# Sinkhorn-sorted block attention and a two-layer dense block: loading one batch at a time, and placing attention inside the second dense layer

## The chip, the cores and the metric

The kernel runs on one core of a Trainium2 chip. The time is what the device needs for one execution, in microseconds (us); three runs gave 297.11, 297.15 and 297.39. Beside these stands one profiled execution, whose trace gives every instruction's start and length. Five engines work side by side: TensorE (PE; matmuls and transposes, with the loading of their weights shown apart as PEld), VectorE (DVE), ScalarE (ACT), GpSimd (POOL) and SyncE (SP). Each has its own queue and waits on the others through semaphores.

## The reference

There are 4 batches of 8 heads with 768 tokens of 64 numbers. A head's tokens form 8 blocks of 96. A small 8x8 matrix per head is exponentiated and normalized along rows and columns, five times (Sinkhorn); it mixes the blocks of k and of v; then each block of queries attends to its mixed block alone. The heads side by side form a 3072 x 512 matrix x that goes through two dense layers.

```python
for _ in range(5):
    P = P - np.max(P, axis=-1, keepdims=True)
    P = np.exp(P)
    P = P / (np.sum(P, axis=-1, keepdims=True) + 1e-09)
    P = P / (np.sum(P, axis=-2, keepdims=True) + 1e-09)
k_sorted = np.einsum('bhij,bhjcd->bhicd', P, k_b)      # v likewise
scores = scale * np.matmul(q_b, k_sb.transpose(0, 1, 2, 4, 3))
attn = softmax(scores)                                  # rows, max taken off
x = (attn @ v_sb), heads side by side                   # 3072 x 512
h = x @ w_in                                            # 512 -> 2048
g = s * (np.maximum(h, 0.0) ** 2) + b
out = g @ w_out                                         # 2048 -> 512
```

## The kernel before

All matmuls take bf16; the loads issued by POOL narrow fp32 to bf16 on the way. The four batches are handled as two groups of two. `load_raw` (L74 on) brings a group's q, k and v in with one partition for each (batch, head, block): 128 partitions, a block's 96 x 64 numbers in each. After group 0 the whole of w_in (L94) and the whole of w_out (L96) are loaded, all on POOL's queue.

The Sinkhorn loop (L123 to L140) alternates between DVE and ACT. `build_pd` spreads the result into `pd`, a 128 x 128 block-diagonal mixing matrix. `transforms(g)` cuts the rest into pieces:

- `qk_piece` (L196): per token offset in a block one pair of matmuls, with the raw rows as weights, turns q (with the identity) and k (with `pd`) into "head dimension on partitions", 64 columns each; the PSUM result is copied to SBUF by `evac`, which alternates DVE (L171) and ACT (L173).
- `v_piece` (L206): per head-dimension index one matmul with 96 weight columns, taken with a stride of 64 elements, and 128 moving columns.

`attention` handles half a batch, 4 blocks of all 8 heads, which is one dense tile of 384 tokens: per pair of heads `s_piece` (scores, L229, exponential on ACT, L233) and `p_piece` (values with a column of ones for the row sum, L248; reciprocal and scaling on DVE, L253 and L254), and last `t_piece` (transposes of x, L265, and a copy to `xt`).

The dense layers: `ffn1(t)` computes 16 chunks of 128 hidden columns, two at a time (L290: 8 matmuls of 384 columns), then relu on ACT (L295) and the square on DVE (L296). `ffn2(t)` computes three blocks of 128 rows, each of 16 matmuls of 512 columns (L304), an output step on DVE (L307) that applies s and the bias, and a store by SP (L310). The bias row is b times the column sum of w_out: POOL adds the 16 slices (L326, L328), one matmul with ones spreads the sum (L330), DVE scales it (L332).

The order: group 0's transforms and its four halves of attention come first, then the bias, then `ffn1(0)`. After it `ffn1(t+1)` and `ffn2(t)` alternate, and a counter of slots (`slot`, one for each pair of chunks and each row block) runs group 1's pieces between them. The program's order is a priority; a scheduler at build time lays out each engine's queue, PE's too, from it. PSUM has two pools, `psa` (3 buffers of two banks) and `psb` (2 buffers of one bank).

Of the kernel before, what the change touches and what calls it, by code (L numbers as in the profile page):

```python
# [13 lines left out]
AX = mybir.AxisListType  # L14


@with_exitstack
def kernel(
# [12 lines left out]
    nc = tc.nc  # L31
# [5 lines left out]
    NG = 2  # L37
    GB = B // NG
# [7 lines left out]
    CH = BLK // 2  # L46
    VW = D + 2
    scale = float(D) ** -0.5

    raw = [t.rearrange("b h (j c) d -> (b h j) (c d)", j=NB) for t in (q, k, v)]  # L50
# [3 lines left out]
    wpool = ctx.enter_context(tc.tile_pool(name="wpool", bufs=1))  # L54
    rawp = ctx.enter_context(tc.tile_pool(name="rawp", bufs=1))
    trp = ctx.enter_context(tc.tile_pool(name="trp", bufs=1))
    atp = ctx.enter_context(tc.tile_pool(name="atp", bufs=4))
    xp = ctx.enter_context(tc.tile_pool(name="xp", bufs=2))
    xtp = ctx.enter_context(tc.tile_pool(name="xtp", bufs=5))
# [10 lines left out]
    nc.scalar.dma_start(out=s_bc, in_=moe_s.to_broadcast([128, 1]))  # L70
    b_bc = const.tile([128, 1], FP)
    nc.scalar.dma_start(out=b_bc, in_=moe_b.to_broadcast([128, 1]))

    def load_raw(g):  # L74
        rows = slice(g * 128, (g + 1) * 128)
        tiles = []
        for t, nm in enumerate("qk"):
            halves = []
            for hf in range(2):
                ti = rawp.tile([128, CH, D], BF, name=f"{nm}b{g}{hf}", tag=f"{nm}b{hf}")  # L80
                nc.gpsimd.dma_start(
                    out=ti.rearrange("p c d -> p (c d)"),
                    in_=raw[t][rows, hf * CH * D:(hf + 1) * CH * D])
                halves.append(ti)
            tiles.append(halves)
        vb = rawp.tile([128, BLK, D], BF, name=f"vb{g}", tag="vb")
        nc.gpsimd.dma_start(out=vb.rearrange("p c d -> p (c d)"), in_=raw[2][rows])
        tiles.append(vb)
        return tiles

    ident = const.tile([128, 128], BF)
    raws = [load_raw(0)]
    wi = wpool.tile([128, NHP, d_ff], BF)
    nc.gpsimd.dma_start(out=wi, in_=moe_w_in.rearrange("(hp p) f -> p hp f", p=128))  # L94
    wo = wpool.tile([128, NF, d_model], BF)
    nc.gpsimd.dma_start(out=wo, in_=moe_w_out.rearrange("(f p) n -> p f n", p=128))  # L96


    make_identity(nc, ident)
    identf = const.tile([128, 128], FP)  # L100
    nc.vector.tensor_copy(out=identf, in_=ident)
# [6 lines left out]
    emat = const.tile([BH, NG * 128], FP)  # L108
    nc.gpsimd.memset(emat, 1.0)
    nc.gpsimd.affine_select(out=emat, in_=emat, pattern=[[1, NG * 128]], base=0,  # L110
                            channel_multiplier=-NB, compare_op=ALU.is_ge, fill=0.0)
    nc.gpsimd.affine_select(out=emat, in_=emat, pattern=[[-1, NG * 128]], base=NB - 1,
                            channel_multiplier=NB, compare_op=ALU.is_ge, fill=0.0)
    onesf = const.tile([128, 128], FP)
    nc.gpsimd.memset(onesf, 1.0)
    jsel = const.tile([128, NB], FP)
    nc.vector.tensor_reduce(out=jsel, in_=identf.rearrange("p (m x) -> p x m", x=NB),
                            axis=AX.X, op=ALU.add)

# [3 lines left out]
    nc.vector.tensor_reduce(out=rstat, in_=sn, axis=AX.X, op=ALU.max)  # L123
    nc.vector.tensor_tensor(out=sn, in0=sn, in1=rstat.broadcast_to([BH, NB, NB]),
                            op=ALU.subtract)
    for it in range(5):
        nc.scalar.activation(out=sn, in_=sn, func=AF.Exp)
        nc.vector.tensor_reduce(out=rstat, in_=sn, axis=AX.X, op=ALU.add)
        nc.vector.reciprocal(out=rrec, in_=rstat)
        nc.vector.tensor_tensor(out=sn, in0=sn, in1=rrec.broadcast_to([BH, NB, NB]),  # L130
                                op=ALU.mult)
# [185 lines left out]
    for p in pieces:  # L317
        p()
# [82 lines left out]
```

## Time and profile before

| | us |
|---|---|
| median of three runs | 297.15 |
| the profiled execution, whole | 297.94 |
| its span, first to last instruction | 295.9 |
| PE busy | 245.7 |
| DVE busy | 117.1 |
| ACT busy | 104.1 |
| POOL busy | 27.9 |
| mean granted PE clock | 0.885 of full |

The page cuts the span into 40 slices of 7.4 us; a digit is the busy share in tenths. A row of a group gives line, engine, operation, output and inputs, shape and count, then busy time and mean length of one, then the idle time of the engine before it and what ended it. Matmuls overlap in the pipeline, so the mean length of one is longer than the distance between two; a distance is read from starts. A row of the timeline begins with the start and the length of a run of like instructions.

### The profile page before, as it was taken

The page shows a single profiled execution, that of the slowest core. Times are in us where ns is not written, and L with a number is a line of the kernel's source. Part 1 is how long each engine was busy: PE and PEld are TensorE (multiplying, and loading weights), DVE is VectorE, ACT ScalarE, POOL GpSimd, SP SyncE. Part 2 cuts the span into 40 slices and gives each one's busy share as a digit, 9 for nine tenths or more (in the row PEclk, how much of TensorE's full clock was granted, in tenths as well). Part 3 has the DMA queues.
Part 4 walks back from the last instruction along what each step waited for, and adds up shares of the span by engine and source line. Part 5 has one row for each costly group of instructions (what it writes and reads, how often), then busy time and mean ns, then how long its engine had stood idle before and what let it go on. Part 6 is the DMA issues. An engine that isn't in the chain of part 4 may idle for free.

```text
span 295.9 us, 5457 instructions
## 1 busy us (share of the span) xinstructions
PE 245.7 (83%) x2421; PEld 155.4 (53%) x2438; DVE 117.1 (40%) x220; ACT 104.1 (35%) x126; POOL 27.9 (9%) x42
## 2 busy tenths in 40 slices
PE   0474982005899999999999999999999999999994
PEld 0373972003675666558864565555465465455441
DVE  4763442003473455433533463434354255324221
ACT  2052261001654656305452364084054155046000
POOL 8100003993000000000000000000000000000000
PEclk9997555555555999999999999999999999999999
DMA  6999994299800000011001100100100110110111
GB/s 94 195 230 199 214 206 78 35 214 219 172 2 0 1 2 4 11 62 38 0 0 38 71 2 32 63 13 2 72 35 2 71 38 0 72 38 0 73 71 71
DMA packets 7847, 20.28 MB, mean 69 GB/s; under 512 B 912, under 2 KB 2960, under 8 KB 7568
## 3 DMA queue, kind: packets, MB, share of 16 engines
q0 software_dynamic: 4032, 13.63, 24.0%
q1 hardware_dynamic: 3504, 6.30, 5.7%
q8 instruction: 19, 0.31, 0.4%
q10 hardware_dynamic: 288, 0.00, 0.1%
q14 instruction: 4, 0.03, 0.0%
HBM read 27.27 MB, written 6.29 MB: 113 GB/s over the span
## 4 chain that ended last, share of the span: by engine, by line
PE 71%; ACT 3%; issue 2%; DVE 1%; ACTq 0%
PE hps L290 28%; PE ops L304 28%; PE tv L206 3%; PE pv L248 3%; PE sc L229 3%; PE tr L265 2%; PE tp L196 2%; ACT at L233 2%; ACT rt L295 1%; PE bps L330 1%; DVE ks L171 0%; DVE ot L307 0%; DVE gt L296 0%; ACT xt L173 0%; ACTq L233 0%
## 5 line engine op out<-in xcount | busy, mean ns | idle before, releaser
L290 PE MATMUL hps<-xt,wi 128*128 128x384 bf16 x512 | 91.5, 330 | 0.5 <-ACT rt L295 0.5
L304 PE MATMUL ops<-wo,gt 128*128 128x512 bf16 x367 | 83.7, 379 | 1.1 <-issue 0.5
L295 ACT ACTIVATE rt<-hps 128x768 bf16<-128x768 f32 x64 | 51.8, 811 | 44.6 <-PE hps L290 42.5
L290 PEld LDWEIGHTS <-wi 128*128 128x128 bf16 x512 | 49.2, 101 | 30.5 <-issue 2.1
L304 PEld LDWEIGHTS <-gt 128*128 128x128 bf16 x384 | 36.4, 98 | 41.8
L296 DVE TENSOR_TENSOR gt<-rt 128x768 bf16<-128x768 bf16 x64 | 35.6, 556 | 49.6 <-ACT rt L295 49.5
L233 ACT ACTIVATE at<-sc 96x768 bf16<-96x768 f32 x32 | 25.5, 805 | 59.6 <-PE sc L229 59.4
L307 DVE SCALAR_TENSOR_TENSOR ot<-ops,s_bc,bias 128x512 f32<-128x512 f32 x24 | 18.0, 751 | 59.1 <-PE ops L304 59.1
L206 PE MATMUL tv<-pd,vb 128*96 128x128 bf16 x128 | 21.7, 343 | 1.2 <-DMA vb<-in_v_dram 1.2
L206 PEld LDWEIGHTS <-vb 128*96 128x96 bf16 x128 | 21.7, 256 | 1.7 <-DMA vb<-in_v_dram 1.3
L254 DVE TENSOR_TENSOR x<-pv,rec 96x512 bf16<-96x512 f32 x32 | 22.0, 686 | 1.1
L330 PE MATMUL bps<-csum,onesf 128*128 128x512 f32 x2 | 2.1, 1140 | 22.9 <-POOL csum L328 22.9
L248 PE MATMUL pv<-vs,at 96*128 96x66 bf16 (+1 forms) x256 | 17.3, 221 | 2.7 <-ACT at L233 2.6
L248 PEld LDWEIGHTS <-at 96*128 96x128 bf16 (+1 forms) x256 | 14.8, 118 | 7.3 <-ACT at L233 3.9
L196 PE MATMUL tp<-ident,qb 128*64 128x64 bf16 x384 | 9.9, 219 | 9.6 <-DMA qb<-in_q_dram 9.4
L328 POOL TENSOR_TENSOR csum<-csum,wo 128x512 f32<-128x512 f32 x14 | 16.2, 1156 | 0.8
L171 DVE CAST vs<-tv 96x1024 bf16<-96x1024 f32 x8 | 9.8, 1221 | 15.9 <-PE tv L206 15.9
L229 PE MATMUL sc<-qt,ks 64*96 64x96 bf16 x256 | 14.7, 249 | 1.1 <-ACT xt L173 0.7
L196 PEld LDWEIGHTS <-qb 128*64 128x64 bf16 x384 | 8.9, 134 | 11.7 <-DMA qb<-in_q_dram 9.4
L229 PEld LDWEIGHTS <-ks 64*96 64x96 bf16 x256 | 10.6, 151 | 7.9 <-issue 6.3
L173 ACT COPY xt<-tr 128x1536 bf16<-128x1536 bf16 x4 | 5.7, 1436 | 22.6 <-PE tr L265 22.6
L330 PEld LDWEIGHTS bps<-csum,onesf 128*128 128x128 f32 x2 | 0.5, 309 | 23.1 <-POOL csum L328 23.1
(50 smaller groups left out, 107.7 us busy)
## 6 DMA issues: line engine op xcount, KB each, us to landing
out_dram<-ot SPq DMA_DIRECT2D x24, 256.0 KB, 2.0
qb<-in_q_dram POOLq DMA_DIRECT2D x4, 768.0 KB, 8.3
kb<-in_k_dram POOLq DMA_DIRECT2D x4, 768.0 KB, 13.6
vb<-in_v_dram POOLq DMA_DIRECT2D x2, 1536.0 KB, 19.6
wi<-in_moe_w_in_dram POOLq DMA_DIRECT2D x1, 2048.0 KB, 34.5
wo<-in_moe_w_out_dram POOLq DMA_DIRECT2D x1, 2048.0 KB, 43.9
s_bc<-in_moe_s_dram ACTq DMA_DIRECT2D x1, 0.5 KB, 3.1
sn<-in_sort_net_dram SPq DMA_DIRECT2D x1, 8.0 KB, 1.6
```

What stands on the lines that cost most here:

```text
L196: nc.tensor.matmul(out=ps[e * 64:(e + 1) * 64, t, :], lhsT=src[:, c1 + t, :], rhs=mov[:, e], start=True, stop=True)
L206: nc.tensor.matmul(out=ps[:, t, :], lhsT=vb[:, :, d0 + t], rhs=pds[g].rearrange("p e m x -> p (e m x)"), start=True, stop=True)
L229: nc.tensor.matmul(out=sc[:, e, n * BLK:(n + 1) * BLK], lhsT=G.ks[pr, g0 + n, :], rhs=G.qt[pr, g0 + n, :], start=True, stop=True)
L233: nc.scalar.activation(out=at, in_=sc[:, :, 0:TG], func=AF.Exp, scale=scale)
L248: nc.tensor.matmul(out=pv[0:m, e, n * VW:(n + 1) * VW], lhsT=atf[:, c0:c0 + m], rhs=G.vs[:, e * 64 + g0 + n, :], start=True, stop=True)
L254: nc.vector.tensor_tensor(out=x[:, :, hp * 128:(hp + 1) * 128].rearrange("p n (e d) -> p e n d", e=2), in0=pvv[:, :, :, 0:D], in1=rec.unsq ...
L290: nc.tensor.matmul(out=hps[:, f, 0:TG], lhsT=wi[:, hp, (f0 + f) * 128:(f0 + f + 1) * 128], rhs=xt[:, hp, :], start=(hp == 0), stop=(hp == ...
L295: nc.scalar.activation(out=rt, in_=hps[:, :, 0:TG], func=AF.Relu)
L296: nc.vector.tensor_tensor(out=gt[:, f0:f0 + 2, :], in0=rt, in1=rt, op=ALU.mult)
L304: nc.tensor.matmul(out=ops, lhsT=gt[:, f, m * 128:(m + 1) * 128], rhs=wo[:, f, :], start=(f == 0), stop=(f == NF - 1))
L307: nc.vector.scalar_tensor_tensor(out=ot, in0=ops, scalar=s_bc, in1=bias, op0=ALU.mult, op1=ALU.add)
L328: nc.gpsimd.tensor_tensor(out=csum, in0=csum, in1=wo[:, f, :], op=ALU.add)
```

## The change

The groups are gone. Batch 0 alone is loaded first, then w_in in four parts, w_out in four parts, and batch 1; k and v of batches 2 and 3 come as a pair of 128 partitions, later. Batches 0 and 1 use 64 partitions of `kb` and `vb` each. q is loaded with 128 partitions of six consecutive tokens per head, and made into `QT` by transposes (`q_piece`). k and v of one batch are mixed by `k_piece1` and `v_piece1`, of the pair by `k_piece2` and `v_piece2`. `vb` has 128 token columns, of which the last 32 are zeros, so that the weights of v's matmuls are 128 columns wide.

PE's queue is in the program's order (`manual_schedule`); the other engines' queues are still laid out by the scheduler, with the Sinkhorn loop given priority. Matmuls on zeros (`warm_up`) stand at PE's start. Only half of batch 0 is attended to before `ffn1(0)`; the second half runs inside `ffn1(0)` in a small form that uses `psb`. The rest runs inside the second dense layer, whose slots now stand after every four matmuls, two tiles at a time: `ffn1(t)`, `ffn1(t+1)`, then `ffn2(t)`, `ffn2(t+1)`. The column sum of w_out is emitted after `ffn1(1)`; outputs that are complete before the bias exists wait in a list (`flush`). The loads of s and b go from ACT's queue to SP's. An activation on a single number stands ahead of the first exponential.

```diff
+    def load_q(b):
+        qr[b] = qrp.tile([128, H, TQ, D], BF, tag="qr", name=f"qr{b}")
+        for h0 in range(0, H, H // 2):
+            nc.gpsimd.dma_start(
+                out=qr[b][:, h0:h0 + H // 2].rearrange("p h t d -> p h (t d)"),
+                in_=q[b, h0:h0 + H // 2].rearrange("h (p t) d -> p h (t d)", t=TQ))
+    def load_k(rows, prow):
+        for c0 in range(0, BLK, CQ):
+            nc.gpsimd.dma_start(out=kb[prow, c0:c0 + CQ, :], in_=kraw[rows, c0:c0 + CQ, :])
+    def load_v(rows, prow):
+        nc.gpsimd.dma_start(out=vb[prow, 0:BLK, :], in_=vraw[rows])
...
+    zt = const.tile([128, 512], BF)
+    nc.vector.memset(zt, 0.0)
+    load_q(0)
+    load_k(*brows(0))
+    load_v(*brows(0))
...
-    wi = wpool.tile([128, NHP, d_ff], BF)
-    nc.gpsimd.dma_start(out=wi, in_=moe_w_in.rearrange("(hp p) f -> p hp f", p=128))
...
+    nc.vector.memset(vb[:, BLK:128, :], 0.0)
+    warm = sk.tile([1, 1], FP)
+    nc.vector.memset(warm, 0.0)
+    nc.scalar.activation(out=warm, in_=warm, func=AF.Exp)
...
+    for c0 in range(0, d_ff, FCH):
+        w = const.tile([128, NHP, FCH], BF, name=f"wi{c0}")
+        nc.gpsimd.dma_start(
+            out=w, in_=moe_w_in.rearrange("(hp p) f -> p hp f", p=128)[:, :, c0:c0 + FCH])
+        wis.append(w)
...
+    load_q(1)
+    load_k(*brows(1))
+    load_v(*brows(1))
...
+    def warm_up(n):
+        for _ in range(n):
+            wp = psb.tile([128, 512], FP, tag="b", name="wp")
+            nc.tensor.matmul(out=wp, lhsT=zt[:, 0:128], rhs=zt, start=True, stop=True)
...
+    def q_piece(b, hp0, n, eng, small=False):
...
+        for i in range(n):
+            for t in range(TQ):
+                for e in range(2):
+                    nc.tensor.transpose(
+                        out=ps[e * 64:(e + 1) * 64, i, t * 128:(t + 1) * 128],
+                        in_=qr[b][:, 2 * (hp0 + i) + e, t, :], identity=ident)
+        evac(QT[b][:, hp0:hp0 + n, :].rearrange("q a (p t) -> q a p t", t=TQ),
+             ps[:, 0:n, 0:S].rearrange("q a (t p) -> q a p t", t=TQ), eng)
+    def k_piece1(b, c0, eng):
+        pr = brows(b)[1]
+        ps = psa.tile([128, CQ, 32], FP, tag="a", name="tk")
+        for c in range(CQ):
+            for e in range(2):
+                nc.tensor.matmul(out=ps[e * 64:(e + 1) * 64, c, :], lhsT=kb[pr, c0 + c, :],
+                                 rhs=pd1[pr, e], start=True, stop=True)
+        g0 = (b % 2) * 32
+        evac(ks[:, g0:g0 + 32, c0:c0 + CQ], ps.rearrange("p c g -> p g c"), eng)
...
+    def v_piece1(b, d0, eng):
+        pr = brows(b)[1]
+        ps = psa.tile([128, 16, 64], FP, tag="a", name="tv")
+        for t in range(16):
+            nc.tensor.matmul(out=ps[:, t, :], lhsT=vb[pr, :, d0 + t],
+                             rhs=pd1[pr].rearrange("p e m i -> p (e m i)"),
+                             start=True, stop=True)
...
+    def v_piece2(d0, eng):
+        ps = psa.tile([128, 8, 128], FP, tag="a", name="tv")
+        for t in range(8):
+            nc.tensor.matmul(out=ps[:, t, :], lhsT=vb[:, :, d0 + t],
+                             rhs=pd2.rearrange("p b e m i -> p (b e m i)"),
+                             start=True, stop=True)
...
+    def s_piece(t, hp, small=False):
...
+        if small:
+            sc = [psb.tile([BLK, 512], FP, tag="b", name="sc") for _ in range(2)]
...
+        if small:
+            for e in range(2):
+                nc.scalar.activation(out=at[:, e], in_=sc[e][:, 0:TG], func=AF.Exp, scale=scale)
...
+    def flush():
+        while waiting:
+            r0, ops = waiting.pop(0)
+            ot = osb.tile([128, d_model], FP, tag="ot", name="ot")
...
                 nc.tensor.matmul(out=ops, lhsT=gt[:, f, m * 128:(m + 1) * 128],
+                                 rhs=wo_at(f), start=(f == 0), stop=(f == NF - 1))
+                if f % 4 == 3:
+                    if f == NF - 1:
+                        waiting.append((t * TG + m * 128, ops))
+                        if ready:
+                            flush()
+                    slot()
...
+        def __call__(self):
+            self.at += 1
+            self.run_to(len(self.pieces) * self.at // self.n)
...
+        if small:
+            return [s(0), s(1), p(0), s(2), p(1), s(3), p(2), p(3), nothing,
+                    lambda: t_piece(t, 0, 2, "v", True), lambda: t_piece(t, 2, 2, "v", True)]
...
+        return [both(s(0), s(1)), nothing, both(p(0), p(1)), both(s(2), s(3)), nothing,
+                both(p(2), p(3)), nothing, lambda: t_piece(t, 0, 4, "s")]
+    with tc.manual_schedule(engines={PE}):
+        warm_up(9)
+        for hp in range(NHP):
+            q_piece(0, hp, 1, "s", small=True)
+        warm_up(6)
...
+        for i, c0 in enumerate(range(0, BLK, CQ)):
+            k_piece1(0, c0, "vsv"[i])
+        v_piece1(0, 0, "s")
+        v_piece1(0, 16, "v")
+        s_piece(0, 0)
+        v_piece1(0, 32, "v")
+        s_piece(0, 1)
+        v_piece1(0, 48, "v")
+        s_piece(0, 2)
+        s_piece(0, 3)
+        for hp in range(NHP):
+            p_piece(0, hp)
+        s_piece(1, 0, small=True)
+        t_piece(0, 0, 4, "s")
+        pt2 = block_rows(1)
...
+        qu = Queue(attn(1, small=True)[1:], 8)
+        ffn1(0, qu)
+        qu.run_to(len(qu.pieces))
+        ffn1(1)
+        csum = const.tile([128, d_model], FP)
+        nc.gpsimd.tensor_tensor(out=csum, in0=wo_at(0), in1=wo_at(1), op=ALU.add)
+        for f in range(2, NF):
+            nc.gpsimd.tensor_tensor(out=csum, in0=csum, in1=wo_at(f), op=ALU.add)
...
+        pieces = [lambda: q_piece(1, 0, 2, "s"), lambda: q_piece(1, 2, 2, "v")]
+        pieces += [lambda i=i: k_piece1(1, i * CQ, "vsv"[i]) for i in range(3)]
+        pieces += [bias_piece]
+        pieces += [lambda i=i: v_piece1(1, i * 16, "svsv"[i]) for i in range(4)]
+        pieces += attn(2) + attn(3)
+        qu = Queue(pieces, 24)
+        ffn2(0, qu)
+        load_q(2)
+        load_k(slice(128, 256), slice(0, 128))
+        load_v(slice(128, 256), slice(0, 128))
+        ffn2(1, qu)
+        load_q(3)
+        qu = Queue([lambda hp=hp: q_piece(2, hp, 1, "v", True) for hp in range(NHP)]
+                   + [lambda c0=c0: k_piece2(c0, "v") for c0 in range(0, BLK, 8)], 16)
+        ffn1(2, qu)
+        ffn1(3, qu)
+        vp = [lambda i=i: v_piece2(i * 8, "svsvsvsv"[i]) for i in range(8)]
+        qu = Queue(vp + attn(4) + attn(5), 24)
+        ffn2(2, qu)
+        ffn2(3, qu)
+        ffn1(4)
+        ffn1(5)
+        qu = Queue([lambda: q_piece(3, 0, 2, "s"), lambda: q_piece(3, 2, 2, "v")]
+                   + attn(6) + attn(7), 24)
+        ffn2(4, qu)
+        ffn2(5, qu)
+        ffn1(6)
+        ffn1(7)
+        ffn2(6)
+        ffn2(7)
```

403 lines of the change are left out of this document (189 added, 214 removed).

## The prediction

> **What bounds the kernel now.** I read the page's slices first, then the busy time by stage, then the groups by line and the timeline where stages change.
>
> ```profile
> span 295.9 us, 5457 instructions
> PE 245.7 (83%) x2421; PEld 155.4 (53%) x2438; DVE 117.1 (40%) x220; ACT 104.1 (35%) x126; POOL 27.9 (9%) x42
> ...
> PE   0474982005899999999999999999999999999994
> ...
> PEclk9997555555555999999999999999999999999999
> ```
>
> TensorE (PE) is saturated from about slice 13 to the end, at full clock. Before that it is part idle and, from slice 4 on, at half clock. Stage by stage (stretch and length, busy time and count per engine, granted clock, DMA share, GB/s):
>
> ```profile
> 0.00:9.43 9.43, 0.00 (x0) 0.00 (x1) 4.69 (x23) 2.30 (x5) 7.68 (x21) 1.00 0.71 106
> 9.43:28.83 19.40, 11.09 (x388) 10.28 (x388) 11.21 (x27) 6.33 (x7) 0.00 (x0) 0.94 1.03 214
> 28.83:39.51 10.68, 10.68 (x64) 10.57 (x64) 4.86 (x4) 3.07 (x3) 0.00 (x0) 0.50 1.09 211
> 39.51:47.50 7.99, 5.77 (x85) 4.84 (x84) 3.58 (x9) 4.81 (x6) 0.00 (x0) 0.50 1.17 196
> 47.50:69.50 22.00, 0.00 (x0) 0.00 (x0) 0.00 (x0) 0.04 (x1) 19.89 (x20) 0.50 0.58 112
> 69.50:90.70 21.20, 18.72 (x233) 14.93 (x234) 12.86 (x27) 10.10 (x12) 0.33 (x1) 0.50 0.52 109
> 90.70:94.20 3.50, 3.50 (x18) 1.93 (x17) 0.31 (x1) 1.56 (x2) 0.00 (x0) 0.50 0.00 0
> 94.20:262.10 167.90, 166.26 (x1489) 98.07 (x1502) 70.62 (x118) 69.36 (x84) 0.00 (x0) 1.00 0.08 29
> ```
>
> The first dense matmul starts only at about 90.8 us: loads and the q/k transforms of two batches (to 28.8), their v transforms (10.7), four halves of attention at half clock, and in their middle 22 us in which only GpSimd (POOL) works. These waits name it:
>
> ```profile
> POOL csum L326 <- DMA wo<-in_moe_w_out_dram: 40.0, 1, 40.0
> ...
> PE bps L330 <- POOL csum L328: 22.9, 1, 22.9
> ```
>
> The column sum of w_out waits for the last load of the queue, and its bias matmul stands in PE's order ahead of attention. So the kernel is about 91 us of start, 201 us of saturated PE, and a tail.
>
> **The prices.** The dense layers, from the groups (busy, mean), one uninterrupted first-layer tile, and two output evictions 16 matmuls apart:
>
> ```profile
> 262.10 10.56 PE L290 MATMUL hps<-xt,wi 128*128 128x384 bf16 x64
> 288.45 0.75 DVE L307 SCALAR_TENSOR_TENSOR ot<-ops,s_bc,bias 128x512 f32<-128x512 f32 x1 [2.70 <-PE ops L304]
> 291.90 0.75 DVE L307 SCALAR_TENSOR_TENSOR ot<-ops,s_bc,bias 128x512 f32<-128x512 f32 x1 [2.70 <-PE ops L304]
> ```
>
> A first-layer tile is 10.4 us less pipeline end (1.30 per chunk of eight), a second-layer row block 3.45, so eight tiles cost 8 x 10.4 + 24 x 3.45 = 166.0. The change leaves all of it. Inserted work, read as start of a piece to start of the dense matmuls behind it, all at full clock:
>
> ```profile
> 104.69 0.69 PE L196 MATMUL tp<-ident,qb 128*64 128x64 bf16 x32
> 105.32 0.99 PE L290 MATMUL hps<-xt,wi 128*128 128x384 bf16 x5
> ...
> 134.14 1.37 PE L206 MATMUL tv<-pd,vb 128*96 128x128 bf16 x8
> 135.35 1.46 PE L290 MATMUL hps<-xt,wi 128*128 128x384 bf16 x8
> ...
> 166.58 0.38 PE L229 MATMUL sc<-qt,ks 64*96 64x96 bf16 x8
> 166.89 1.47 PE L290 MATMUL hps<-xt,wi 128*128 128x384 bf16 x8
> 168.20 0.43 PE L248 MATMUL pv<-vs,at 96*128 96x66 bf16 x8
> 168.47 1.47 PE L290 MATMUL hps<-xt,wi 128*128 128x384 bf16 x8
> ...
> 171.34 0.85 PE L265 MATMUL tr<-ident,x 96*128 96x96 bf16 x16
> 172.03 0.65 PE L290 MATMUL hps<-xt,wi 128*128 128x384 bf16 x3
> ```
>
> So a 32-matmul q/k piece is 0.63 (20 ns each), eight v matmuls 1.21 (151 each), scores 0.31, values 0.27, the transposes 0.69. A half batch of attention is 4 x 0.31 + 4 x 0.27 + 0.69 = 3.0 us of PE.
>
> These prices rebuild the old saturated part: 166.0 + 4 x 3.0 + 12 x 0.63 + 8 x 1.21 = 195.2, plus 1.7 for the 3.5 us at half clock, 197; measured 90.8 to 291.9 is 201. 4 us are stalls that no price covers.
>
> **The change, part by part.** *Start.* Only batch 0 is loaded ahead. The stretch of 214 GB/s counts landed bytes:
>
> ```profile
> 28.83 10.75 PE L206 MATMUL tv<-pd,vb 128*96 128x128 bf16 x64 [1.16 <-DMA vb<-in_v_dram]
> ...
> qb<-in_q_dram POOLq DMA_DIRECT2D x4, 768.0 KB, 8.3
> wi<-in_moe_w_in_dram POOLq DMA_DIRECT2D x1, 2048.0 KB, 34.5
> wo<-in_moe_w_out_dram POOLq DMA_DIRECT2D x1, 2048.0 KB, 43.9
> ```
>
> Two batches of q, k, v are 4.72 MB and were in at 28.8; at 214 GB/s that is 22.0, so 6.8 us go on start-up and completion. One batch (2.36 MB, 11.0) is then in at 17.8, its q at 10.5 and k at 14.2; w_in (9.8 more) at 27.6, w_out at 37.4, batch 1 at 48.4. Splitting w_in and w_out into four loads each costs issue time on POOL's queue only. The s and b loads go from ACT's queue to SP's, behind the sort matrix; SP has nothing else until the first output.
>
> ```profile
> 12.16 0.21 DVE L140 TENSOR_TENSOR sn<-sn,rrec 32x64 f32<-32x64 f32 x1
> ...
> 13.53 2.19 PE L196 MATMUL tp<-ident,qb 128*64 128x64 bf16 x74
> 14.09 0.63 DVE L160 TENSOR_TENSOR pd<-bmask,pt 128x64 bf16<-128x64 f32 x4
> ```
>
> The Sinkhorn loop ends at 12.4 as before; one mask instead of two gives 13.9, near k's 14.2. The added memsets on DVE and q copies on ACT share those engines with the loop: 0 to 2 us, I take 0, since the loop is given priority. The 15 warm-up matmuls lie before data arrives and cost nothing while it is late; without that cover, 15 x 0.43 (twice 3.45/16) = 6 us at half clock.
>
> Per batch, k takes 192 matmuls of 32 columns. They are not in the trace; nearest is the 64-column piece: 29 ns (2.19/74, early and slow) or 20 ns. So 3.8 to 5.6, done at 18.0 to 19.8, v arriving meanwhile. For v, 64 loads of weights are padded from 96 to 128 columns. Bounds: 34 ns (the eight value matmuls, whose weights are 128 wide but contiguous) and 151 x 128/96 = 201 (strided as now). The wide contiguous load, at most 34 ns, against a 96-wide contiguous score pair (0.31/4 = 78 ns) is 0.27 against 0.81 ns per column, a third; a third of 201 is 67. I take 65: 4.2 us for a batch or, after that, for the pair of batches. With four score pieces between and one eviction behind, v ends at about 25 (full clock) to 27.5. Then the four value pieces go at VectorE's pace and one copy ends it:
>
> ```profile
> L254 DVE TENSOR_TENSOR x<-pv,rec 96x512 bf16<-96x512 f32 x32 | 22.0, 686 | 1.1
> L173 ACT COPY xt<-tr 128x1536 bf16<-128x1536 bf16 x4 | 5.7, 1436 | 22.6 <-PE tr L265 22.6
> L295 ACT ACTIVATE rt<-hps 128x768 bf16<-128x768 f32 x64 | 51.8, 811 | 44.6 <-PE hps L290 42.5
> L296 DVE TENSOR_TENSOR gt<-rt 128x768 bf16<-128x768 bf16 x64 | 35.6, 556 | 49.6 <-ACT rt L295 49.5
> L328 POOL TENSOR_TENSOR csum<-csum,wo 128x512 f32<-128x512 f32 x14 | 16.2, 1156 | 0.8
> ```
>
> 4 x 0.93 (with the reciprocal's 0.2) + 0.8 + 1.4: the first tile stands at 31 to 33.6, I take 32. w_in is there by then.
>
> *After it*, on PE: 166.0 dense; seven halves of attention 21.0; q of three batches by 48 transposes each, 1.4 (two at a time) to 2.7 (43 ns x 128/96 each), take 2.0, 6.0; k of batch 1 and of the last pair 192 x 20 ns each, 7.7; v likewise 4.2 twice, 8.4; the bias matmul 1.5 (2.1 at half clock); half clock at the first dense matmuls 1.7, as before. Sum 212.3.
>
> *Covers.* Attention costs only its PE time if ACT and DVE keep up: the first pair of second-layer tiles (20.7 dense, 17.6 inserted) asks of ACT 8 x 0.81 + 2.9 + 4.5 = 14 us and of DVE 8 x 0.89 + 6 x 0.75 + 5.8 = 17.5, of 38. The 22 us wait is not moved elsewhere: csum needs 17.4 us of POOL after w_out's first quarter (30), ends by about 50, and its matmul stands near 67; the outputs held back until then are two, which two buffers hold. Batch 1 is in 13 us before its use. The last pair's loads stand behind csum on POOL and behind batch 1's transforms, about 80; 4.72 MB are 22 us, needed from 100 (q first) on.
>
> *The new waits.* PE's order is fixed, so a late piece stops the dense matmuls behind it, and ACT and DVE behind those. The tight place is the first dense tile, with the small form of attention: its scores and its values each take both buffers of pool `psb`. A pair of pieces is serial, 0.31 + 1.0 (two exponentials) + 0.27 + 1.1 (two DVE pairs) and handovers, about 3.1 to 4.5, when a relu of 0.81 stands ahead, against 3.2 us of two slots: 0 to 4 us over it all, take 3. For the rest the old 4.
>
> Sum: 32 + 212.3 + 7 = 251.3; from PE's end to the span's, 4.0 (295.9 - 291.9); 255.3. Outside the span lie 2.0 (297.94 profiled), so 257.3 for a profiled run; the shown median, 297.15, lies 0.8 below its own, so 256.5. I say 256.
>
> **Rivals.** (1) *v stays slow.* If the strided, padded loads gain nothing, 201 ns, three times 8.7 us more: 282; at 151, 272. For it: the 151 hardly changes at half clock (10.68/64 = 167), so the load, not the matmul, sets it. Against: the wide contiguous loads run three times faster. [...] (3) *csum now runs beside VectorE's squares.* If each square first waits out a csum addition (1.16 + 0.56 per 1.30 us chunk), 14 chunks lose 0.42, about 6 us, and the small attention some more: 263. In the old trace DVE was at 0.00 during csum. [...] (4) *Slower*: the clock falls where small pieces cut the dense stream. Stage 69.50 had PE 88% busy and stayed at 0.50. If the three interleaved second-layer stretches (38 + 31 + 29 us) ran so, they would add up to 98: 354; from 41 us of it on, slower than now. Against: 94.20 to 262.10 interleaves the same pieces at 1.00. (5) *The order does nothing much but the start is better*: full clock through the start, no new stalls: 30 + 212 - 2 + 3 + 6 - 1 = 248 or less.
>
> **How the numbers follow.** Forecast with its own range 247 to 266 (bounds: start 30 to 35, v 34 to 100 ns, stalls 2 to 11): 0.66, which takes in (2) and most of (3) alone; (1) 0.13; (2) and (3) together or worse waits, 266 to 275, 0.08; (5) below 247, 0.08; (4) 0.04; the remaining 0.01 is a wash. The range 244 to 275 leaves out (4), the worst of (1) and a little below. Runs of this kernel agree within 0.1%, so 0.2% tells a change: faster 0.95, same 0.01, slower 0.04.
>
> **What would show it.** [...] No PE wait on POOL. The v group's mean spacing 50 to 80 ns (200: rival 1). Squares of 0.56 that grow or start late while csum runs: rival 3. Clock 1.00 from some 4 us into the dense part (0.50 later: rival 4). Second-layer stretches of 38, 31 and 29 us; longer with PE waiting on ACT or DVE means the fixed order costs more than I gave. I am wrong if PE's idle time after the first dense matmul exceeds 12 us.

## The result, and the profile after

The changed kernel takes 0.915 of the time before, 95% interval 0.904 to 0.926: 270.1 and 273.9 us in two runs, against a median of 297.3 for the kernel before on the same chip. Two more runs, 275.5 (the profiled one) and 276.1, with a mean granted clock of 0.92 and 0.91 where the first two show 1.00 and 0.99, count as slow and are left out of the ratio. So what is read from the profile below is compared, where it can be, with an experiment that leaves that part of the kernel alone.

The profile page of the changed kernel: span, busy time by engine, PE's slices and the granted clock in them.

```profile
span 273.8 us, 5666 instructions
...
PE 250.0 (91%) x2517; PEld 149.4 (55%) x2517; DVE 123.3 (45%) x238; ACT 103.6 (38%) x129; POOL 40.0 (15%) x58
...
PE   5486579798998999999999999999999999999994
...
PEclk9675556889997979999999999999999999999999
```

PE's saturated part now starts at slice 7 (of 6.8 us here) instead of 13. The clock is low in slices 2 to 9, lowest in 4 to 6, and it falls again in slices 13 and 15. By stage (stretch and length, busy time and count of PE, PEld, DVE, ACT, POOL, clock, DMA share, GB/s):

```profile
0.00:41.38 41.38, 26.05 (x412) 19.85 (x413) 19.58 (x56) 13.09 (x20) 21.39 (x40) 0.65 1.08 181
41.38:61.98 20.60, 18.23 (x136) 10.39 (x136) 9.90 (x27) 8.94 (x14) 14.95 (x13) 0.80 0.61 112
61.98:73.02 11.04, 10.57 (x64) 6.27 (x65) 4.51 (x9) 5.68 (x7) 0.00 (x0) 1.00 0.01 1
73.02:117.86 44.84, 43.27 (x564) 25.92 (x562) 18.40 (x30) 12.65 (x14) 3.68 (x6) 0.92 0.57 119
117.86:146.64 28.78, 28.78 (x373) 16.63 (x370) 18.83 (x31) 13.78 (x17) 0.00 (x0) 1.00 0.03 11
146.64:178.83 32.19, 32.19 (x325) 20.45 (x321) 16.73 (x28) 12.02 (x14) 0.00 (x0) 1.00 0.11 42
178.83:199.64 20.81, 20.81 (x133) 12.53 (x131) 8.34 (x16) 13.52 (x16) 0.00 (x0) 1.00 0.04 13
199.64:228.05 28.41, 28.41 (x306) 15.54 (x305) 13.34 (x25) 9.61 (x11) 0.00 (x0) 1.00 0.13 48
228.05:269.70 41.65, 41.65 (x228) 21.82 (x225) 12.95 (x22) 14.32 (x17) 0.00 (x0) 1.00 0.10 38
```

The rows are the start, `ffn1(0)`, `ffn1(1)`, `ffn2(0)` and `(1)`, and so on in pairs. The first dense matmul moved from 90.8 to 41.4, and PE's last one from 291.9 to 269.7: the start gave 49 us and the saturated part took 27 back. By the prediction's prices some 15 of the 27 are work that now lies in it, three more of the eight half batches of attention and batch 1's transforms; the rest is taken up stretch by stretch below.

The place where the start is held, from PE's timeline (first five rows, the last being the first dense matmul), and GpSimd's timeline beside it:

```profile
13.06 2.94 PE L160 MATMUL wp<-zt 128*128 128x512 bf16 x6 [0.19 <-ACT qt L209]
15.93 0.43 PE L192 MATMUL pe<-sn,emat 32*128 32x64 f32 x2
...
23.21 1.09 PE L236 MATMUL tk<-pd,kb 64*64 64x32 bf16 x35 [2.82 <-issue]
...
35.44 2.29 PE L310 MATMUL pv<-vs,at 96*128 96x66 bf16 x32 [4.05 <-POOL vs L149]
...
41.38 2.72 PE L361 MATMUL hps<-xt,wi 128*128 128x384 bf16 x8 [0.91 <-ACT xt L209]
```

```profile
8.62 0.75 POOL L113 DMA_DIRECT2D wi<-in_moe_w_in_dram  x1 [1.50 <-DMA qr<-in_q_dram]
...
19.02 0.75 POOL L135 DMA_DIRECT2D wo<-in_moe_w_out_dram  x1 [3.07 <-DMA vb<-in_v_dram]
...
34.54 0.52 POOL L90 DMA_DIRECT2D vb<-in_v_dram  x1 [1.99 <-DMA wo<-in_moe_w_out_dram]
35.05 0.34 POOL L149 MEMSET vs<- 96x256 bf16 x1
```

PE waits 4.05 us for a memset of ones on GpSimd (`vs` L149, the column that makes the row sums). The memset itself takes 0.34. It stands in GpSimd's queue behind 20 loads (7 in the old kernel, where it ran at 8.4), and GpSimd's rows show loads after the eighth waiting for earlier ones to land: at 8.62, eight (two of q, three of k, one of v, two of w_in) are in flight, and the ninth goes out when q's lands. Of the twelve later loads ahead of the memset nine wait so, 1.02 to 3.07 us each, and by the names in these waits each goes out only when the load issued eight before it has landed. The last one ahead of the memset goes out at 34.54.

### The profile page after: what moved, and what is told of

It reads as the page before. It is cut to its first block, busy times and chain, and to the rows that moved or that the text cites. A ratio compares the mean times of both kernels' runs of the same rounds, so it can differ in the third digit from the quotient of the medians.

```text
span 273.8 us, 5666 instructions
## 1 busy us (share of the span) xinstructions
PE 250.0 (91%) x2517; PEld 149.4 (55%) x2517; DVE 123.3 (45%) x238; ACT 103.6 (38%) x129; POOL 40.0 (15%) x58
## 4 chain that ended last, share of the span: by engine, by line
PE 81%; DMA 10%; DVE 4%; POOL 2%; issue 1%; ACT 1%; POOLq 0%
PE hps L361 32%; PE ops L386 32%; DMA wo<-in_moe_w_out_dram 7%; DMA qr<-in_q_dram 3%; PE sc L283 3%; PE pv L310 3%; PE tv L255 2%; PE tv L264 2%; PE tq L224 2%; PE tr L342 2%; PE tk L246 2%; DVE x L325 1%; PE tk L236 1%; DVE gt L366 1%; ACT rt L365 1%
## 5 line engine op out<-in xcount | busy, mean ns | idle before, releaser
L386 PE MATMUL ops<-wo,gt 128*128 128x512 bf16 x384 | 93.5, 386 | 0.0
L365 ACT ACTIVATE rt<-hps 128x768 bf16<-128x768 f32 x64 | 51.9, 812 | 44.8 <-PE hps L361 43.8
L366 DVE TENSOR_TENSOR gt<-rt 128x768 bf16<-128x768 bf16 x64 | 36.6, 572 | 38.3 <-ACT rt L365 38.2
L377 DVE SCALAR_TENSOR_TENSOR ot<-ops,s_bc,bias 128x512 f32<-128x512 f32 x24 | 17.9, 747 | 31.0 <-PE ops L386 31.0
L290 ACT ACTIVATE at<-sc 96x768 bf16<-96x768 f32 x28 | 21.2, 803 | 24.0 <-PE sc L283 24.0
L207 DVE CAST ks<-tk 128x512 bf16<-128x512 f32 (+1 forms) x16 | 13.2, 825 | 18.0 <-PE tk L236 10.8
L209 ACT COPY xt<-tr 128x1536 bf16<-128x1536 bf16 x7 | 10.1, 1439 | 23.7 <-PE tr L342 23.7
L209 ACT CAST vs<-tv 96x1024 bf16<-96x1024 f32 x7 | 7.2, 1025 | 25.1 <-PE tv L255 17.6
L310 PE MATMUL pv<-vs,at 96*128 96x66 bf16 (+1 forms) x256 | 12.7, 203 | 4.2 <-POOL vs L149 4.0
L324 DVE RECIPROCAL rec<-pv 96x8 f32<-96x8 f32 x28 | 5.2, 194 | 23.0 <-PE pv L310 23.0
L255 PEld LDWEIGHTS <-vb 64*128 64x128 bf16 x128 | 12.0, 216 | 1.7 <-issue 1.7
L224 PE MATMUL tq<-ident,qr 128*64 128x128 bf16 x192 | 8.2, 237 | 4.9 <-DMA qr<-in_q_dram 3.1
L236 PE MATMUL tk<-pd,kb 64*64 64x32 bf16 x384 | 8.0, 187 | 5.1 <-issue 4.2
## 6 DMA issues: line engine op xcount, KB each, us to landing
wi<-in_moe_w_in_dram POOLq DMA_DIRECT2D x4, 512.0 KB, 17.9
wo<-in_moe_w_out_dram POOLq DMA_DIRECT2D x4, 512.0 KB, 20.1
```

Source lines behind the costliest of these rows:

```text
L207: nc.vector.tensor_copy(out=out, in_=in_)
L209: nc.scalar.copy(out=out, in_=in_)
L255: nc.tensor.matmul(out=ps[:, t, :], lhsT=vb[pr, :, d0 + t], rhs=pd1[pr].rearrange("p e m i -> p (e m i)"), start=True, stop=True)
L290: nc.scalar.activation(out=at, in_=s2[:, :, 0:TG], func=AF.Exp, scale=scale)
L310: nc.tensor.matmul(out=pv[e][0:m, n * VW:(n + 1) * VW], lhsT=atf[:, c0:c0 + m], rhs=vs[:, gi, :], start=True, stop=True)
L365: nc.scalar.activation(out=rt, in_=hps[:, :, 0:TG], func=AF.Relu)
```

## The experiments

They ask five things: what holds the start; where the later stretches lost time; whether the padding of v works; where the gain comes from; and what a better version would be. T0 below is the start of the first dense matmul.

**The ones ahead of the loads.** The memsets of `vs`'s ones and of `onesf` moved ahead of the loads of w_in, nothing else.

```diff
+    vs = const.tile([BLK, 128, VW], BF)
+    nc.gpsimd.memset(vs[:, :, D:VW], 1.0)
+    onesf = const.tile([128, 128], FP)
+    nc.gpsimd.memset(onesf, 1.0)
     wis, wos = [], []
```

> The memsets of v's ones column and of the ones matrix stand ahead of the w_in loads on POOL's queue; all else as changed. Theory P (POOL's queue is what made the start late: the memset stood behind loads that wait for earlier loads to land, and PE waited 4.0 us for it): the first value matmul starts near 31.5 instead of 35.4, the first dense matmul near 37.4, and the time falls by about 4 us. Rival C (the start is set by the clock and the late v, the memset only came last among several): the first dense matmul moves by under 1.5 us and the time by under 1 us.

```profile
31.84 2.29 PE L310 MATMUL pv<-vs,at 96*128 96x66 bf16 x32 [0.64 <-DVE vs L207]
37.78 2.72 PE L361 MATMUL hps<-xt,wi 128*128 128x384 bf16 x8 [0.91 <-ACT xt L209]
```

T0 is 37.78, and the wait on POOL is gone from the value matmuls. T0 is 41.38 in the profile of the changed kernel, and 40.59, 40.67 and 41.00 in the three experiments below that leave the start alone, so here the memset's place cost 2.8 to 3.6 us of the start; with the next run, which has the ones early too and T0 at 38.71, the bounds are 1.9 and 3.6. The granted half clock of the start is not what held it: in the experiment with the sum on PE the clock is 1.00 through the whole start (0.987 over the whole run), and T0 is 40.59. The whole run is 271.9 us (ratio 0.915, 0.912 to 0.918), inside the spread of the unmoved kernel; only the stage shows the gain.

**The masks ahead too.** The memsets and selects that make `bmask`, `emat` and `hmask` moved there as well.

> As the run before it, and the masks are also built ahead of the w_in loads, so that the mixing matrix does not wait for them (they ended at 13.7). Theory W (the second warm-up of six matmuls, which ends at 15.9, holds PE's fixed order, not the masks): mixing matrix still at 17.2, no gain over the run before it (within 0.5 us). Rival M (masks): mixing matrix near 14 and 3 us gained.

271.0 us (0.913, 0.911 to 0.916), T0 38.71: no gain at the start. The masks did not hold the mixing matmul; it started at 16.53, right behind the six warm-up matmuls:

```profile
16.53 0.59 PE L192 MATMUL pe<-sn,emat 32*128 32x64 f32 x2
```

**No second warm-up.** The last kernel without `warm_up(6)`.

```diff
             q_piece(0, hp, 1, "s", small=True)
-        warm_up(6)
```

> As the run before it, without the second warm-up. Theory W: the matmul for the mixing matrix starts near 12.8 instead of 15.9, k's pieces near 14.2; but v lands only near 19, so v's pieces start near 19.5 to 21 instead of 24.2, and the first dense matmul comes 2 to 4 us sooner, near 33 to 35. Rival (v's landing and a stop for instructions set it): under 1 us sooner. Rival H (the warm-up keeps the clock up): k and v pieces run slower without it and the gain is lost.

269.8 us (0.906, 0.903 to 0.910). PE's timeline of this kernel:

```profile
13.50 0.65 PE L192 MATMUL pe<-sn,emat 32*128 32x64 f32 x2 [0.25 <-issue]
15.05 4.51 PE L236 MATMUL tk<-pd,kb 64*64 64x32 bf16 x163 [0.90 <-DVE pd L436]
21.22 0.93 PE L236 MATMUL tk<-pd,kb 64*64 64x32 bf16 x29 [1.66 <-issue]
...
29.86 2.29 PE L310 MATMUL pv<-vs,at 96*128 96x66 bf16 x32 [0.64 <-DVE vs L207]
...
35.80 0.80 PE L361 MATMUL hps<-xt,wi 128*128 128x384 bf16 x2 [0.91 <-ACT xt L209]
```

The mixing matmul comes 3.0 earlier and T0 2.9 earlier, at 35.8; against the run with the ones alone both come 2.1 and 2.0 earlier. The warm-up stood in PE's fixed order behind q's evictions and ahead of the mixing matmul, and its own time (2.7 to 3.2 us) was on the path. It bought no clock that lasted either: the first dense tile is 20.1 us without it and 20.3 with it.

**The column sum on PE.** The changed kernel without GpSimd's 15 additions; instead, 16 bf16 matmuls with ones add the slices of w_out in PSUM.

```diff
-        csum = const.tile([128, d_model], FP)
-        nc.gpsimd.tensor_tensor(out=csum, in0=wo_at(0), in1=wo_at(1), op=ALU.add)
-        for f in range(2, NF):
-            nc.gpsimd.tensor_tensor(out=csum, in0=csum, in1=wo_at(f), op=ALU.add)
...
-            nc.tensor.matmul(out=bps[:, 0], lhsT=onesf, rhs=csum, start=True, stop=True)
+            for f in range(NF):
+                nc.tensor.matmul(out=bps[:, 0], lhsT=onesb, rhs=wo_at(f),
+                                 start=(f == 0), stop=(f == NF - 1))
```

> The changed kernel with the column sum of w_out done by 16 accumulating PE matmuls of 512 columns in the bias piece, and none on POOL. Theory L (POOL's additions held up VectorE's squares, which then held up the small attention in the first dense tile): squares in that tile are back at 0.56 us each, and the tile shrinks from 20.6 us to 18 to 19; the first pair of second-layer tiles grows by 2.0 (3.45 against 1.5). Time: 0 to 2 us less. Rival (the small attention's two buffers and the cold clock alone set it): the tile stays within 0.7 us of 20.6 and the time rises by about 2 us.

`ffn1(0)` took 17.9 us. With the sum on GpSimd it took 20.6 in the profile after, 20.6, 20.3 and 20.1 in the three experiments above, and 19.3 in the one with pairs below. VectorE's squares in that stretch, from the groups, first with the sum on PE, then in the changed kernel, then in the kernel with pairs (busy, mean ns):

```profile
L366 DVE TENSOR_TENSOR gt<-rt 128x768 bf16<-128x768 bf16 x8 | 4.5, 557 | 5.4 <-ACT rt L365 5.1
```

```profile
L366 DVE TENSOR_TENSOR gt<-rt 128x768 bf16<-128x768 bf16 x8 | 5.6, 694 | 4.6 <-ACT rt L365 4.5
```

```profile
L366 DVE TENSOR_TENSOR gt<-rt 128x768 bf16<-128x768 bf16 x8 | 7.0, 880 | 4.2 <-ACT rt L365 4.0
```

557 ns alone, 694 to 880 beside GpSimd's additions (1,068 in the kernel with the ones moved, 1,160 in the one without the second warm-up). A part of the stretch's gain is clock: it was 1.00 here and 0.80 in the profile after. At 0.92 in both, the kernel with pairs takes 19.3 and the one with this edit and the three above takes 17.5, 1.8 us less, though their starts differ. The kernel with those three edits and the sum still on GpSimd, which has the same start, takes 20.1 at a clock of 0.90. So 1.8 to 2.6 us are the sum's. The stretch at 0.92 in the two, in that order:

```profile
40.67:59.99 19.32, 15.72 (x137) 9.44 (x136) 11.26 (x27) 8.96 (x14) 15.09 (x13) 0.92 0.71 129
```

```profile
35.70:53.20 17.50, 15.67 (x137) 9.42 (x137) 8.32 (x26) 8.85 (x14) 1.54 (x2) 0.92 1.15 199
```

In the whole run no gain can be seen: 273.2 us (0.921, 0.916 to 0.926). The 16 matmuls take longer than the two they replace: `ffn2(0)` and `(1)` went from 44.8 in the changed kernel to 46.6, with 6.8 us at half clock in both.

**No padding.** v's weights 96 columns wide instead of 128.

```diff
-            nc.tensor.matmul(out=ps[:, t, :], lhsT=vb[pr, :, d0 + t],
+            nc.tensor.matmul(out=ps[0:BLK, t, :], lhsT=vb[pr, 0:BLK, d0 + t],
```

> The changed kernel, but v's matmuls take 96 weight columns instead of 128 with 32 zeros. Theory (padding is what makes the strided weight load fast): in the stretch of the second pair of second-layer tiles v's eight matmuls take 1.2 us again instead of 0.70, batch 1's sixteen near 2.4 instead of 1.55; the stretches grow by 4 and 3.4 us and the time by 7 to 10. Rival (they are fast for other reasons, such as fewer rows or columns): batch 1's stay near 1.55, the pair's near 0.70, the time stays.

283.2 and 288.1 us. A piece of batch 1's v from start to the dense matmuls behind it, in PE's timeline, first padded (changed kernel), then not:

```profile
88.53 1.62 PE L255 MATMUL tv<-pd,vb 64*128 64x64 bf16 x16
90.08 1.04 PE L386 MATMUL ops<-wo,gt 128*128 128x512 bf16 x4
```

```profile
89.62 2.82 PE L255 MATMUL tv<-pd,vb 64*96 64x64 bf16 x16
92.38 1.03 PE L386 MATMUL ops<-wo,gt 128*128 128x512 bf16 x2
```

1.55 against 2.76 us for 16, 97 against 172 ns for one; the pair's eight take 0.70 against 1.22, 88 against 152 each. The matmuls with the wider weights follow each other faster. But at 88 to 97 ns the strided ones are not as fast as the contiguous ones, for which the prediction's rows bound 34 ns.

**No late loads.** k and v of batches 2 and 3 are not loaded; those batches use k and v of batches 0 and 1.

> The changed kernel with the loads of k and v of batches 2 and 3 left out (those batches then use the k and v of batches 0 and 1). Theory F (PE's idle 1.35 us at 82.7 in the third k piece is a fetch of instructions that queues behind those loads): the idle time goes, the four dense matmuls behind it take 0.96 instead of 1.69, and the stretch of the first pair of second-layer tiles falls from 44.8 to about 42. Half clock at the end of v's pieces (97.7 to 101) stays if the thin k and v matmuls cause it, goes if the loads do. Rival: nothing changes, the loads have no part in it.

276.7 (the profiled run) and 272.1 us. The stop of PE in batch 1's k is 1.35 us in the changed kernel and 0.75 here, still beside the loads of q. But it is 0.72 to 0.85 also in six kernels with all loads, so the shorter stop is not owed to the missing loads. The rows of the changed kernel, of this one, and of the kernel without the second warm-up:

```profile
84.08 0.40 PE L236 MATMUL tk<-pd,kb 64*64 64x32 bf16 x9 [1.35 <-issue]
84.23 0.30 PE L236 MATMUL tk<-pd,kb 64*64 64x32 bf16 x9 [0.75 <-issue]
78.07 0.21 PE L236 MATMUL tk<-pd,kb 64*64 64x32 bf16 x3 [0.84 <-issue]
```

The half clock stayed: 0.51 from 94.7 to 101.6, with PE busy 95% of the time and no DMA at all, as the stretch's row shows.

```profile
94.70:101.60 6.90, 6.57 (x49) 3.89 (x50) 1.22 (x1) 1.36 (x2) 0.00 (x0) 0.51 0.00 0
```

So half clock there needs no running transfer (the same is seen in a run with all loads, in the last section). What part the loads have in the stop this run does not tell.

**The kernel before, its sum emitted later.** In the old kernel, the block that adds the column sum and multiplies it by ones is written after `ffn1(0)`. The first run did this alone.

> The kernel before, with one edit: the column sum and the bias matmul are written after the first dense tile instead of ahead of it, and so stand later in PE's order. Theory (the 22 us in which PE waited for the sum are most of what the change gained, the rest of its gain at the start is given back later): PE goes on with attention at 47.5, the first dense matmul comes near 69, the saturated part stays at 201 us, time 274 to 278, the same as the changed kernel. Rival (loads of the second group or the sum become late for the dense part, and the gain needs the new order): over 285.

297.3 us, ratio 0.999 (0.998 to 1.001), and the wait stayed, by the timeline of this kernel:

```profile
69.33 2.07 PE L361 MATMUL bps<-csum,onesf 128*128 128x512 f32 x2 [22.77 <-POOL csum L359]
```

The scheduler laid the bias matmul at the same place in PE's queue, so this told nothing of what the wait costs. The second run also puts PE's queue in the program's order, as the change does.

```diff
+    with tc.manual_schedule(engines={PE}):
         build_pd(0)
         build_pd(1)
...
         ffn1(0, nothing)
+        csum = const.tile([128, d_model], FP)
+        nc.gpsimd.tensor_tensor(out=csum, in0=wo[:, 0, :], in1=wo[:, 1, :], op=ALU.add)
```

> The kernel before with the column sum written after the first dense tile, and PE's queue in the program's order (the only way in which the edit reaches PE: laid out by the scheduler, the bias matmul stayed where it was). Theory G (most of the change's gain is the 22 us in which PE waited for the sum): no PE wait on POOL, the first dense matmul near 69 to 73 (the mixing matrix now stands ahead of q, which costs up to 3), the saturated part 201 to 206, time 275 to 283. Rival N (the gain needs the one-batch start; here other waits take the place, as the fixed order stalls attention on its exponentials): first dense matmul after 80 or a saturated part over 212, time over 288.

277.4 us, ratio 0.931 (0.929 to 0.934). PE's timeline, and the granted clock by slices of 6.9 us:

```profile
68.75 11.84 PE L291 MATMUL hps<-xt,wi 128*128 128x384 bf16 x64
80.43 1.02 PE L363 MATMUL bps<-csum,onesf 128*128 128x512 f32 x2
```

```profile
PEclk9997555555899999999999999999999999999999
```

T0 went from 90.8 to 68.75 and the bias matmul waits for nothing. About 20.5 of the change's 25.3 us (ratios 0.931 and 0.915 of 297.3) are had without a new load, a new transform or attention in the second layer. The fixed order came with the edit and was not run alone; but T0 moved by 22.05, the length of the wait, and the saturated part is 203 us instead of 201, so it is the wait that was gained. The start is still 68.75 long, at half clock from 23.6 on, and yet the end comes only 5 us later than with the whole change: what the change takes out of the start, beyond the wait, is mostly time that comes back in the saturated part, 228 us there and 203 here.

**Pieces in pairs.** In `ffn1(2)` and `(3)` of the changed kernel, two pieces after every second chunk instead of one after each.

```diff
+        def every_other():
+            qu.at += 1
+            if qu.at % 2 == 0:
+                qu.run_to(qu.at)
-        ffn1(2, qu)
-        ffn1(3, qu)
+        ffn1(2, every_other)
+        ffn1(3, every_other)
```

> The changed kernel, where in the stretch of the third and fourth first-layer tiles two pieces follow every second chunk instead of one piece every chunk. The stretch was 28.8 us in each run so far. Theory I (each place where small matmuls cut the dense stream costs about 0.1 us beside the piece itself, once per place): eight places fewer, 28.0 us. Rival S (the 0.1 belongs to each piece): 28.8. Rival B (two pieces in a row wait for PSUM): over 29.

The stretch with the same work went from 28.8 to 27.6 us with eight cuts fewer, 0.15 each (271.8 and 270.6 us in all). Its rows, and the two pieces of timeline in the changed kernel that say why:

```profile
115.39:142.96 27.57, 27.04 (x373) 16.84 (x370) 19.00 (x32) 14.31 (x17) 0.00 (x0) 1.00 0.03 11
```

```profile
126.71 0.44 PE L246 MATMUL tk<-pd,kb 128*64 128x64 bf16 x16
127.08 1.48 PE L361 MATMUL hps<-xt,wi 128*128 128x384 bf16 x8
128.49 0.44 PE L246 MATMUL tk<-pd,kb 128*64 128x64 bf16 x16
```

A chunk of eight between two pieces takes 1.41 (127.08 to 128.49); uninterrupted it is 1.30. So each cut costs 0.11 us ahead of the piece, in time in which PE is shown busy.

**No second warm-up and the sum on PE together.**

> Ones and masks ahead of the w_in loads, no second warm-up, and the column sum by 16 PE matmuls: the edits of three runs together. First dense matmul near 35.8, first dense tile 17.9 to 18.5, first pair of second-layer tiles 44 to 46.6, the rest as always (170.8 to the span's end): span 265 to 268, time 267 to 270. Rival: the edits share their gain (the sum beside the first tile was only in the way because the tile came early): time as without the sum on PE, 269.8 or more.

269.0 us (0.904, 0.901 to 0.906); T0 35.7, `ffn1(0)` 17.5, and then 46.1 for the first second-layer pair, with 6.8 us at half clock from 86.4 on.

**Batch 1's thin pieces spread out.** From that kernel, q and k of batch 1 move into `ffn1(1)`, which had nothing inserted, and v's pieces are halved and take twice the slots. The PE work is the same.

```diff
+        qu = Queue([lambda: q_piece(1, 0, 2, "s"), lambda: q_piece(1, 2, 2, "v")]
+                   + [lambda i=i: k_piece1(1, i * CQ, "vsv"[i]) for i in range(3)], 8)
-        ffn1(1)
+        ffn1(1, qu)
...
-        pieces += [lambda i=i: v_piece1(1, i * 16, "svsv"[i]) for i in range(4)]
+        pieces += [lambda i=i: v_half1(1, i * 8, "svsvsvsv"[i]) for i in range(8)]
```

> The run before it, and batch 1's q and k pieces moved into the second first-layer tile, its v pieces halved and spread over twice as many slots. Theory T (the granted clock falls to half when thin matmuls, 64 rows or 32 to 64 columns, take over half of PE's time for some microseconds, as in the first pair of second-layer tiles of every run so far): no stretch at half clock after the first dense tile; the two stretches together take 11.0 + 46.6 less 2 to 4 us, time 263 to 267. Rival V (v's thin matmuls alone bring the clock down, however they are spread, or waits do): half clock stays, time within 1 us of the run before it.

266.5 us, ratio 0.895 (0.893 to 0.897), and the four runs lie within 0.7 us; the last kernel had 0.904 (0.901 to 0.906). The granted clock (slices of 6.6 us), and the stretches `ffn1(1)` and `ffn2(0)` with `(1)`:

```profile
PEclk9555559999999999999999999999999999999999
```

```profile
53.30:69.80 16.50, 16.03 (x305) 10.52 (x306) 7.78 (x12) 8.88 (x10) 2.57 (x4) 1.00 0.50 81
69.80:108.10 38.30, 38.09 (x340) 21.74 (x337) 15.12 (x29) 9.70 (x13) 1.06 (x2) 1.00 0.45 105
```

After T0's first few us the clock does not fall again. 16.5 + 38.3 = 54.8 stands against 11.0 + 46.1 = 57.1.

**Spread, and in pairs.** The last kernel with the pairs as well.

> The spread version with the pairs of pieces in the third and fourth first-layer tiles. If the cost per cut adds to the rest, that stretch falls from 28.8 to 27.6 us and the time from 266.5 to 265 to 265.6. Rival: two pieces in a row delay the relu and the squares behind them, and the time stays within 0.5 us of 266.5.

265.7 us, ratio 0.895 (0.893 to 0.897): the best version here. The pairs' stretch is 27.6 again, but the two ratios cannot be told apart; in the profiled run `ffn1(0)` and `(1)` took 1.5 us more than in the last kernel, with half clock until further into the first tile.

## Why the prediction was right, and where its steps were not

The sign and the range held: 256 was said for 270.1 and 273.9, inside 244 to 275 (the two longer runs, 275.5 and 276.1, lie just outside). The forecast's own range, 247 to 266, did not: of a gain of 41 us it got 25, and the time fell into the band from 266 to 275, which had a chance of 0.08. The main step, the 22 us wait, was right; that the range held all the same is in part luck, since nearly every miss below lies on the same side. The sums come out as they stand, but for the 33.6 at which the first tile was to stand at the latest (27.5 + 5.9 is 33.4). Stretch by stretch, the prediction's prices against the profile after, and against experiments that leave that stretch alone (sum on PE for the start; pairs for the others):

| stretch | from the prediction's prices | profile after | in the experiment |
|---|---|---|---|
| start | 32.0 | 41.4 | 40.6 |
| `ffn1(0)`, small attention | 18.1 | 20.6 | 19.3 |
| `ffn1(1)` | 10.4 | 11.0 | 11.0 |
| `ffn2(0)`, `(1)` | 38.3 | 44.8 | 44.4 |
| `ffn1(2)`, `(3)` | 26.6 | 28.8 | |
| `ffn2(2)`, `(3)` | 30.9 | 32.2 | |
| the rest | 91.0 | 90.9 | |
| stalls without a place | 4.0 | | |
| PE's end | 251.3 | 269.7 | |

**The start: the step on GpSimd's queue failed.** The prediction said that splitting w_in and w_out "costs issue time on POOL's queue only", and among its signs "no PE wait on POOL". With eight loads in flight, the ninth and most later ones waited for landings, 1.02 to 3.07 us each, and what stood behind them on GpSimd waited too. The memset of the ones, already in the old kernel behind 7 loads and now behind 20, was counted at nothing; it cost 1.9 to 3.6. The second failed step is the warm-up, whose matmuls were to "lie before data arrives and cost nothing while it is late": by the second six, data was not late any more, and they cost 2.0 to 2.9. T0 is 35.8 without both. Of the 3.8 left to 32, 2 are v's matmuls (64 of 97 ns instead of 65) by price, and 1.7 is the stop in k's; this split is read from rows and was not tested.

**v: right mechanism, size short.** The padding works and rival 1 (201 or 151 ns) is refuted; 97 and 88 ns instead of 65, still inside the bounds of 34 to 201. For three times 64 matmuls that is 5.5 us more in all.

**Batch 0's loads of 64 partitions, (2) in the chances, did not come late.** The load that waits for `vb` goes out at 19.02, so v of batch 0 had landed by then; the prediction had worked out 17.8 at the 214 GB/s of the old trace. Other loads were in flight beside these, though, so the rate of one alone is not shown.

**The column sum beside the squares (rival 3) is real.** It was priced at 6 us as a rival; taking the sum away shortened the first tile by 1.8 to 2.6, and left the squares at 557 ns, against 556 in the old trace. That each square waits out a whole addition, as the rival had it, was not shown: with the ones moved the squares' mean of 1,068 ns is 511 above the 557, beside additions of 1,257.

**The clock (rival 4) partly.** The later interleaved stretches ran at 1.00, as said; a 354 us run was refuted. But in `ffn2(0)` and `(1)` the clock was at 0.50 twice for 3.4 us, first from the stop of 1.35 in k's matmuls on, then from the end of batch 1's last v piece on. What it costs can be read from kernels with the same work there: the stretch took 42.5 us with 3.4 at half clock (masks ahead), and 44.9, 44.3 and 44.4 with 10.2 (ones ahead, no second warm-up, pairs), so 0.27 to 0.36 us for each us at half clock. The 6.8 us of the changed kernel then cost about 1.8 to 2.5; with the stop of 1.35, and 2 us for v's dearer pieces, that is most of the 6.5 us lost there. Spreading the same pieces took 2.3 us off and 6.8 us at half clock with it, in line with this. The stretch with the masks ahead and with the ones ahead:

```profile
70.07:112.53 42.46, 41.49 (x564) 25.32 (x562) 18.41 (x30) 12.64 (x14) 3.66 (x6) 0.96 0.60 125
69.35:114.28 44.93, 43.97 (x564) 25.89 (x562) 18.41 (x30) 12.64 (x14) 3.67 (x6) 0.89 0.57 119
```

**Cuts.** The prediction read a piece's price as its start to the dense matmuls behind it, and left 4 us of old stalls "that no price covers". Each cut costs 0.11 to 0.15 us besides: 16 cuts of `ffn1(2)` and `(3)` are about 2 us, the miss in that stretch. That the old kernel's 4 us are the same cost is likely and was not tested.

**What held.** The 22 us wait on GpSimd is gone and was not moved: 20.5 us by itself in the old kernel. The dense layers' price, batch 1 and the last pair in time, and ACT and DVE as cover: the stretches from `ffn1(4)` on came within 0.1 us of their sum. By the stages, PE idled 2.37 + 0.47 + 1.57 = 4.4 us after the first dense matmul, under the 12 given as the mark.

**Open.** Why PE stops for 1.5 to 3.2 us in the middle of k's matmuls at the start, in the changed kernel (2.82) and in nine of its variants (the kernel before has such stops too, of 1.16 and 3.22). The wait is shown as "issue". In the changed kernel it lies from 20.4 to 23.2; the view of DMA queues for 20.0 to 23.3 (queue and kind: packets, MB, share of 16 engines) has one packet that carries instructions, beside full data queues:

```profile
q0 software_dynamic: 670, 0.67, 122.6%
q8 instruction: 1, 0.02, 1.8%
```

That PE's own instructions come late behind the bulk loads fits this, but was not shown: no experiment took the loads from beside a stop. Open too is what brings the half clock in `ffn2(0)` and `(1)`, the thin matmuls or the stop, since spreading the pieces changed both (PE's idle time there fell from 1.1 to 0.2); in the kernel with pairs the clock fell at 88.1, 6.5 us after the stop had ended.

## What to carry to other kernels

Here a queue that issues loads held back what stood behind the ninth of them (nine waits of 1.02 to 3.07 us, and a memset at 35.05 that had run at 8.4): put small work that a later stage needs ahead of the loads, not behind them, and look for it by the engine's own timeline, not by the length of its instructions. Where one wait dominates the old profile, remove it alone first; here it was four fifths of the gain of a rewritten kernel. Pieces inserted into a dense stream cost here, beside their time, 0.11 to 0.15 us for each cut, so eight cuts fewer saved 1.2; and moving thin pieces into a dense stretch that had none saved 2.3, though more and smaller ones were made of them.

## What the runs showed of the hardware

- After eight loads, nine of the next twelve on GpSimd waited 1.02 to 3.07 us, each for the one issued eight before it to land. Whether the chip sets this limit or the program as it was built, no run here shows.
- A PE that is shown busy can be at half clock with no transfer running. The time at half clock in `ffn2(0)` and `(1)` came out near 3.4, 6.8 or 10.2 us (13.6 in the kernel without padding). A stretch of the kernel with pairs:

```profile
92.00:95.00 3.00, 3.00 (x19) 1.61 (x19) 0.00 (x0) 1.01 (x1) 0.00 (x0) 0.50 0.00 0
```

The clock fell at 88.1; PE's whole idle time in the 9 us before this stretch is 0, and the longest stop in the 12 us before it 0.84. So here it fell with no longer stop in those 12 us.
- Matmuls with strided weights of 128 columns follow each other at 88 to 97 ns, with 96 columns at 152 to 172. The clock hardly matters: in the changed kernel's rows 30 of batch 0's v matmuls take 2.90 us at 0.50 and 16 of batch 1's 1.62 at 1.00, 97 and 101 ns each.
- Small matmuls of another shape inside a dense stream cost 0.11 to 0.15 us for each cut beside their own time, and that time shows as busy.
